# Another order of the operations of the first 48 steps in a chunked-attention and two-layer rational/ReLU² feed-forward kernel

## The chip, the cores and the metric

The kernel runs on one core of one Trainium2 chip. The metric is the device time of one execution in microseconds. TensorE is called PE in the profile, VectorE DVE, ScalarE ACT, GpSimd POOL and SyncE SP. SP does no arithmetic here: it issues loads and stores. ACT issues a few loads too, on a queue of its own.

## The reference

Attention within chunks of 64 rows over 8 batches, 8 heads, 576 positions and 64 dimensions; its output is laid out as 4608 tokens of 512 values. Then two feed-forward layers with 2048 hidden values each.

```python
scores = scale * np.matmul(q_c, k_c.transpose(0, 1, 2, 4, 3))     # chunks of 64 x 64
scores = scores - np.max(scores, axis=-1, keepdims=True)
attn = np.exp(scores)
attn = attn / (np.sum(attn, axis=-1, keepdims=True) + 1e-09)
out = np.matmul(attn, v_c)
x = out.transpose(0, 2, 1, 3).reshape(B * S, H * D)               # 4608 x 512
h = x @ w_in                                                      # first layer
P = a[0] + a[1] * h + a[2] * h2 + a[3] * h3
Q = 1.0 + np.abs(b[0]) * np.abs(h) + np.abs(b[1]) * h2
x = (P / (Q + 1e-6)) @ w_out
r = np.maximum(x @ w_in2, 0.0)                                    # second layer
result = (s * (r * r) + b2) @ w_out2
```

The feed-forward weights arrive as 64-bit floating-point numbers and are turned into 32-bit ones on the chip.

## The kernel before

Every product of two float32 matrices is made from a high and a low half of each factor, in three terms. The tokens are cut into nine tiles of 512 (x tiles). Attention is worked in tiles of 128 tokens, four to an x tile. A step of the first layer takes one x tile and 128 of the hidden values: 12 matmuls of 128x512 into one PSUM bank (`mm1`, lines 530 to 532, token M), the rational function on that bank (ACT, DVE, POOL), and 12 matmuls into the x tile's four accumulators (`mm2`, line 548, token R). Steps 0 to 7 belong to x tile 0, steps 8 to 15 to x tile 1, then 16 steps of tile 2, 8 more of tile 1 and 8 more of tile 0. Step i uses bank i mod 3 (`h_bank`), so M of a step needs the last read of the step three before it, which is its operation Nc. Some of attention's transposes and products take those same banks, or the accumulators' banks, which the first R (R0) needs empty.

The order in which instructions are issued is a list of tokens written out by hand in the program (`START`, lines 33 to 82), played by `play`: each token calls one function and each engine carries out its own tokens in the order of the list. `START` covers the first 48 steps with everything that must come ahead of them; `LOOP` and `TURN` and a planner follow and aren't touched. The tokens, with the number of the tile, weight or step:

- loads: P (q and k of an attention tile, 2 DMAs), L and o (v, 4 DMAs), Q (q and k in another layout, 16 DMAs), w (the next weight block, 512 KB), x (parameters). On SP, or on ACT's queue where the token ends in A.
- attention tile: T transposes of q and k on PE, then q and k (ACT copies them out); or X, a turn on DVE. S scores (PE); sa to sd maxima and subtractions (DVE); e exponential (ACT); ma, mb, mc sum and reciprocal (DVE); n norm (POOL, or DVE with D); A transposes (PE), a copy (ACT); V product with v (PE); v high half of x (ACT), u low half (DVE). The small letter behind T, S, A, V chooses the banks.
- weight block n: f starts the conversion (ACT: absolute value `w_abs`, line 445, and low word `w_low`, line 449); gPa to gPd on DVE for two blocks together (lines 456, 460, 463); c sum (POOL, line 466); d high half (ACT, line 473); D or G low half (DVE or POOL, line 477). A weight's staging buffer is one of four in turn, so load n+4 waits for c of block n.
- step: M; t, B, p (ACT), r (POOL or DVE), ba, bb (DVE), l and E (ACT: logarithm and exponential), Na, Nb, Nc (DVE), H high half (ACT), y low half (POOL, or DVE with D), R.

Of the kernel before, what the change touches and what calls it, by code (L numbers as in the profile page):

```python
# [139 lines left out]
def tile_chunk_attention__then__rational_ffn__then__relu2_ffn(  # L140
# [1227 lines left out]
    with tc.manual_schedule():  # L1368
# [24 lines left out]
        words, pairs = {}, {}  # L1393
# [219 lines left out]
```

## Time and profile before

| what | us |
|---|---|
| median of 3 runs | 1640.9 (1638.43 to 1640.9) |
| profiled execution, time | 1639.77 |
| profiled execution, span from first to last instruction | 1638.0 |
| PE busy | 1586.5 (97%) |
| DVE busy | 1338.1 (82%) |
| ACT busy | 1128.0 (69%) |
| POOL busy | 608.8 (37%) |

The page cuts the span into 40 slices of about 41 us; each digit is the busy share of a slice in tenths. A timeline row gives start, length, engine, line of the program, operation, output and inputs, and in brackets the idle time ahead of it with what ended that. Rows of SPq and ACTq are issues of DMAs: the length is how long the issuing engine was held.

### The profile page before, as it was taken

How to read it: one execution, taken by the hardware profiler on the slowest of the kernel's cores; microseconds unless marked ns; L12 is line 12 of the kernel's file. 1: busy time of each engine (PE TensorE's matmuls, PEld its weight loads, DVE VectorE, ACT ScalarE, POOL GpSimd, SP SyncE). 2: the span in 40 equal slices, each digit the busy share in tenths (PEclk: the TensorE clock that was granted, in tenths of full speed). 3: DMA queues.
4: the chain of work that ended last, by engine and by line, in shares of the span. 5: the costliest groups of instructions: out<-in, count | busy, mean ns of one | idle time of the engine just before them, and what ended most of it. 6: DMA issues, size and time to landing. Idle time of an engine off the chain costs nothing.

```text
span 1638.0 us, 26407 instructions
## 1 busy us (share of the span) xinstructions
PE 1586.5 (97%) x9068; PEld 1293.9 (79%) x9068; DVE 1338.1 (82%) x2165; ACT 1128.0 (69%) x1909; POOL 608.8 (37%) x513
## 2 busy tenths in 40 slices
PE   4699999999999999999999999999999999999998
PEld 3577887777878888888888788888888888888886
DVE  6899988899888988888779987668867886788676
ACT  5788766667677686867678776657665756676554
POOL 3677565347577676757557510000000000000000
PEclk9799999999999999999999999999999999999999
DMA  9655302344263553625034587865589649666853
GB/s 232 158 158 147 93 1 65 84 113 134 66 167 87 154 141 83 196 65 133 3 123 135 206 272 238 324 231 174 164 208 303 233 130 297 213 220 161 279 169 86
DMA packets 365526, 263.93 MB, mean 161 GB/s; under 512 B 276816, under 2 KB 315728, under 8 KB 364880
## 3 DMA queue, kind: packets, MB, share of 16 engines
q1 hardware_dynamic: 352720, 255.55, 53.0%
q10 hardware_dynamic: 12672, 6.69, 1.5%
q8 instruction: 72, 1.18, 0.3%
q14 instruction: 62, 0.51, 0.1%
HBM read 201.33 MB, written 60.82 MB: 160 GB/s over the span
## 4 chain that ended last, share of the span: by engine, by line
PE 79%; DVE 6%; DMA 4%; ACT 4%; issue 3%; POOL 2%; SPq 2%; ACTq 0%; DVEq 0%; POOLq 0%
PE acc L548 20%; PE ae L1107 16%; PE hA L1046 11%; PE h L530 7%; PE h L532 6%; PE h L531 6%; PE hE L1046 5%; PE hc L1046 3%; PE hc L1107 3%; DMA wst<-in_moe_w_in_dram 1%; SPq L269 1%; DMA vs<-in_v_dram 1%; PE pat L383 1%; DVE ah L679 1%; PE pat L408 1%
## 5 line engine op out<-in xcount | busy, mean ns | idle before, releaser
L1107 PE MATMUL ae<-gs,wo 128*128 128x512 f32 x1152 | 294.0, 391 | 1.7 <-DVE acc L1126 0.7
L548 PE MATMUL acc<-gh,w 128*128 128x512 f32 x1152 | 288.0, 392 | 0.0
L530 PE MATMUL h<-xh,w 128*128 128x512 f32 x640 | 256.1, 400 | 8.9 <-DVE t L683 8.0
L1107 PEld LDWEIGHTS ae<-gs,wo 128*128 128x128 f32 x1152 | 215.8, 188 | 49.5 <-DVE acc L1126 1.1
L531 PE MATMUL h<-xl,w 128*128 128x512 f32 x640 | 251.0, 392 | 0.0
L532 PE MATMUL h<-xh,w 128*128 128x512 f32 x640 | 251.0, 392 | 0.0
L548 PEld LDWEIGHTS acc<-gh,w 128*128 128x128 f32 x1152 | 214.1, 188 | 44.4 <-ACT gh L691 0.2
L637 POOL TENSOR_TENSOR r<-r,ah 128x512 f32<-128x512 f32 x130 | 174.3, 1341 | 77.6 <-ACT r L632 65.0
L1046 PE MATMUL hA<-xs,wi 128*128 128x512 f32 x768 | 195.6, 390 | 0.7 <-ACT g L1057 0.7
L697 POOL TENSOR_TENSOR gl<-t,gh 128x512 fp32r<-128x512 f32 x111 | 147.7, 1333 | 100.0 <-ACT gh L691 58.4
L1046 PEld LDWEIGHTS hA<-xs,wi 128*128 128x128 f32 x768 | 144.1, 188 | 31.8 <-ACT g L1057 1.1
L1085 DVE TENSOR_TENSOR gs<-g,gs 128x512 fp32r<-128x512 f32 x224 | 146.4, 684 | 15.1 <-ACT gs L1081 14.5
L548 PE MATMUL acc<-gl,w 128*128 128x512 f32 x576 | 154.8, 390 | 2.0 <-POOL gl L697 1.9
L1081 ACT ACTIVATE gs<-g 128x512 fp32r<-128x512 f32 x224 | 132.7, 624 | 28.2 <-DVE g L1077 27.8
L530 PEld LDWEIGHTS h<-xh,w 128*128 128x128 f32 x640 | 121.2, 189 | 39.1 <-DVE t L683 12.4
L532 PEld LDWEIGHTS h<-xh,w 128*128 128x128 f32 x640 | 121.0, 189 | 26.0
L531 PEld LDWEIGHTS h<-xl,w 128*128 128x128 f32 x640 | 121.2, 189 | 24.2 <-DVE xl L424 0.3
L623 ACT ACTIVATE t<-h,a_sb 128x512 f32<-128x512 f32 x144 | 111.1, 773 | 38.1 <-PE h L532 18.1
L548 PEld LDWEIGHTS acc<-gl,w 128*128 128x128 f32 x576 | 107.6, 188 | 26.5 <-POOL gl L697 4.2
L679 DVE SCALAR_TENSOR_TENSOR ah<-r,h 128x512 f32<-128x512 f32 x144 | 98.1, 681 | 37.1 <-ACT h L668 35.7
L1128 DVE TENSOR_TENSOR acc<-ae,acc 128x512 f32<-128x512 f32 x112 | 77.0, 689 | 61.3 <-PE ae L1107 60.3
L663 ACT ACTIVATE ah<-r,lnb 128x512 f32<-128x512 f32 x144 | 103.6, 719 | 32.8 <-POOL r L637 26.5
(143 smaller groups left out, 2964.9 us busy)
## 6 DMA issues: line engine op xcount, KB each, us to landing
wi<-wq SPq DMA_DIRECT2D x112, 512.0 KB, 4.3
wo<-wq SPq DMA_DIRECT2D x112, 512.0 KB, 4.8
wst<-in_moe_w_in_dram SPq DMA_DIRECT2D x28, 512.0 KB, 5.3
wst<-in_moe_w_out_dram SPq DMA_DIRECT2D x27, 512.0 KB, 4.7
wi<-wp SPq DMA_DIRECT2D x16, 512.0 KB, 4.0
wq<-wc SPq DMA_DIRECT2D x32, 256.0 KB, 2.8
w<-wi SPq DMA_DIRECT2D x16, 512.0 KB, 6.6
raw<-x2d SPq DMA_DIRECT2D x16, 512.0 KB, 7.4
```

The source lines that it names most:

```text
L530: T.matmul(h, wh, xh[:, kk], start=kk == 0, stop=False)
L531: T.matmul(h, wh, xl[:, kk], start=False, stop=False)
L532: T.matmul(h, wl, xh[:, kk], start=False, stop=kk == KD - 1)
L548: T.matmul(o, l, r, start=first and n == 0, stop=last and n == 2)
L623: A.activation(t1, h_t[i], AF.Identity, scale=a_sb[:, 3:4], bias=a_sb[:, 2:3])
L637: eng.tensor_tensor(out=r, in0=r, in1=ah, op=ALU.mult)
L679: V.scalar_tensor_tensor(out=t, in0=r, scalar=ONE, in1=y, op0=ALU.add, op1=ALU.mult)
L697: (eng or (G if i < N1 else V)).tensor_tensor(out=gl, in0=tmp.pop(i)["g"], in1=f(g_t[i][0]), op=ALU.subtract)
L1046: T.matmul(ps[b], w[:, l, z * P:(z + 1) * P], x[:, z], start=n == 0 and p in (1, 2, 5), stop=n == 5, skip_group_check=True)
L1081: A.activation(gx[t, s, k][0][:, 0], gt[t, s, c], AF.Copy)
L1085: V.tensor_tensor(out=g[:, 1], in0=gt[t, s, c], in1=f(g[:, 0]), op=ALU.subtract)
L1107: T.matmul(o, w[:, e, l, dp * P:(dp + 1) * P], gx[t, 2 * u + e, k][0][:, g], start=n == 0 and p in (1, 2, 5), stop=n == 5, skip_group_chec ...
```

## The change

The list `START` is replaced by another. Both name the same operations on the same data. The new one begins with attention tiles 2, 3, 4, 0, 1 where the old one begins with 4, 1, 3, 2, 5, 0. It puts other loads on ACT's queue (w0, w9, w10, L2, L4, L0, P3, P6, P7 where the old one has w1, w6, w27 to w30, L1, L3, L2 and P7), and chooses anew which steps' and tiles' n, r, y, D and G run on which engine, and which banks attention's products use. A new token, h with a letter b, does the low word `w_low` of a weight block by itself; f then does the absolute value alone. For the second layer's weights f does both, as before. The heads of both lists, up to some tokens behind R3:

```diff
-    "w0 w1A f0 P4 w2 f1 P1 g1Pa g1Pb g1Pc c0 d0 T4a L1A T1x q1 k1 g1Pd D0 f2 S1y s1b c1 d1 w3 q4 s1d s1a k4 w4 w5 "
-    "f3 P3 S4b s1c e1 s4b g3Pa g3Pb s4d T3d G1 g3Pc g3Pd m1a c2 m1b m1c P2 f4 c3 n1D f5 w6A d2 g5Pa P5 q3 s4a g5Pb "
-    "P0 d3 s4c w7 g5Pc x0 e4 m4a g5Pd A1a k3 T2b c4 c5 a1 V1a S3x q2 s3b k2 d5 s3a d4 G3 s3c S2b s3d e3 w8 v1 D4 "
-    "s2b L4 u1 T5d s2a G2 k5 G5 q5 L3A T0x q0 w9 s2c k0 S5a m4b S0x m4c s2d s5a n4 s5b f6 m3a P6 m3b A4d a4 s5c w10 "
-    "s0a m3c s0b s5d f7 V4d s0d L0 g7Pa n3 f8 g7Pb g7Pd s0c e2 e5 A3b m5a P7A e0 f9 a3 g7Pc v4 T6b m0a q6 m5b g9Pa "
-    "m5c V3c k6 c6 g9Pb n5D m2a w11 g9Pc m0b u4 m0c w12 n0D w13 Q8 c8 A5b S6a s6b L5 L2A c7 L6 T7b w14 d6 a5 w15 "
-    "m2b d7 v3 m2c k7 q7 g9Pd s6a c9 s6d s6c e6 D7 m6a A0d u3 a0 d8 w16 Q9 d9 n2 S7b m6b G6 A2a a2 V2a s7a m6c f10 "
-    "v2 u2 V0c v0 L7 G8 f11 u0 M0 w17 f12 g11Pa o8 M1 o9 g11Pb w18 f13 g11Pc G9 g11Pd t0 n6 c11 w19 g13Pa B0 c10 p0 "
-    "r0h Q10 A6c d11 M2 s7b w20 b0a g13Pb t1 B1 p1 W0 b0b X8 b1a l0 V5a r1h E0 g13Pc s7c c12 s7d b1b e7 t2 S8b M3 "
-    "N0a d10 l1 d12 s8a G11 a6 G12 m7a v5 B2 N0b f14 m7b E1 D10 N0c m7c b2a u5 n7 A7x b2b g13Pd r2 H0 s8b V6a M4 "
-    "N1a s8d y0 f15 N1b v6 s8c l2 N1c t3 u6 H1 c13 g15Pa E2 b3a Q11 R0 B3 d13 N2a e8 a7 y1 g15Pb N2b D13 M5 N2c r3 "
-    "B4 X9 p4 r4h t4 b3b R1 l3 M6 g15Pc g15Pd c14 H2 l4 y2 E3 f16 b4a N3a f17 b4b E4 N3b V7y c15 B5 p5 r5h m8a d14 "
-    "G14 N3c g17Pa H3 t5 d15 B6 l5 y3 v7 R2 N4a N4b m8b t6 N4c g17Pb o10 b5a m8c b5b E5 n8 u7 g17Pd A8c c17 p6 r6h "
-    "N5a a8 H4 N5b w21A M7 f18 l6 Q12 B7 f19 d17 S9y o11 D15 N5c g17Pc y4D c16 H5 s9a b6a s9c g19Pa b6b G17 s9b E6 "
-    "R3 d16 p7 r7h g19Pb t7 y5D M8 g19Pc R4 t8 N6a b7a N6b s9d B8 X10 G16 l7 b8a N6c f20 f21 r8 o12 R5 g19Pd M9 c19 "
...
+    "w0A P2 w1 L2A T2d P3A k2 q2 w2 S2b w3 f0 f1 T3b s2a s2c h1b s2b s2d e2 g1Pa h0b P4 g1Pb m2a k3 f2 q3 g1Pc f3 "
+    "m2b m2c S3a h2b c0 n2D A2c a2 V2x g3Pa d0 s3a h3b g1Pd v2 T4b g3Pb P0 u2 c1 T0d g3Pd d1 s3b s3c s3d G0 w4 D1 "
+    "q4 k4 S4y w5 c3 k0 e3 q0 f4 f5 h5b P6A g3Pc s4b g5Pa s4d d3 g5Pb s4a P1 P5 s4c T1c e4 g5Pd D3 m3a x0 w6 S0b "
+    "T5d s0b s0a s0c s0d k1 q1 h4b m4a c2 d2 k5 T6a P7A q5 c5 S1x w7 m4b d5 k6 G2 m3b g5Pc w8 f6 m4c q6 n4D s1a s1b "
+    "s1c c4 S5x s1d d4 w9A G5 L3 f7 m3c g7Pa s5a g7Pb e1 n3D h6b L4A G4 g7Pc A4d e0 f8 h7b h8b Q8 a4 g7Pd m0a s5b "
+    "c6 c7 m0b m1a s5c f9 s5d A3y V4y m0c m1b w10A e5 g9Pa d7 a3 L0A V3a g9Pb m1c g9Pd n0D w11 g9Pc c8 n1D L1 h9b "
+    "v3 m5a A0b d6 a0 d8 w12 c9 G7 G6 d9 m5b w13 v4 V0a L5 Q9 A1b u3 w14 w15 v0 L6 X8 u4 T7x D8 w16 w17 a1 m5c f10 "
+    "n5 f11 w18 q7 V1b o8 v1 A5x k7 u0 h11b a5 f12 g11Pa S6a G9 h10b u1 g11Pb f13 g11Pd g11Pc c11 c10 w19 h12b s6b "
+    "M0 s6a s6d M1 t0 g13Pa s6c b0a B0 V5y e6 g13Pb S7a S8b p0 r0h o9 m6a L7 w20 B1 p1 b0b m6b g13Pc t1 v5 l0 E0 "
+    "m6c h13b d10 r1h c12 b1a d11 Q10 u5 b1b g13Pd l1 s8a M2 E1 t2 B2 N0a n6 s7b N0b N0c c13 N1a G10 H0 s7d d13 G11 "
+    "A6c f14 f15 h15b b2a N1b W0 s7a G13 N1c s7c H1 p2 r2h g15Pa e7 y0D g15Pb b2b X9 M3 m7a t3 M4 B3 y1 l2 p3 r3h "
+    "a6 Q11 E2 d12 V6a g15Pc v6 b3a f16 o10 l3 b3b m7b B4 N2a Q12 m7c s8b N2b N2c f17 E3 g15Pd G12 u6 s8d t4 n7 "
+    "h16b h14b N3a r4 A7x s8c N3b g17Pa c14 b4a c15 N3c M5 h17b l4 e8 R0 H2 b4b m8a y2D B5 R1 E4 p5 r5h t5 g17Pb H3 "
+    "N4a b5a m8b g17Pd g17Pc N4b l5 d14 a7 y3D c17 b5b d15 N4c M6 c16 m8c B6 t6 p6 r6h E5 b6a H4 n8 R2 y4 d16 G16 "
+    "d17 b6b D14 M7 l6 R3 w21A f18 f19 E6 t7 B7 N5a D15 N5b N5c V7c f20 N6a D17 R4 N6b v7 A8y f21 h20b N6c u7 H5 M8 "
...
```

```diff
-    def w_ends(st, w):
-        w_abs(st, w)
-        w_low(st)
...
-            w_ends(st, w)
+            w_abs(st, w)
+            if phase:
+                w_low(st)
...
-        do["h"] = lambda n, _: w_get(n)
+        do["h"] = lambda n, x: w_low(words[n][3]) if x else w_get(n)
```

## Rows read from the trace of the kernel before

**Rows 1.** The page: busy time of each engine, and PE in tenths of 40 slices
```profile
PE 1586.5 (97%) x9068; PEld 1293.9 (79%) x9068; DVE 1338.1 (82%) x2165; ACT 1128.0 (69%) x1909; POOL 608.8 (37%) x513
...
PE   4699999999999999999999999999999999999998
```

**Rows 2.** Busy time by stretch: stretch, length, each engine, clock, DMA share, GB/s
```profile
0.00:20.00 20.00, 6.62 (x80) 4.76 (x80) 5.83 (x13) 9.53 (x17) 4.82 (x9) 1.00 1.02 245
20.00:60.84 40.84, 24.85 (x425) 19.40 (x425) 36.58 (x76) 28.28 (x58) 22.93 (x18) 0.80 0.80 202
60.84:96.79 35.95, 29.53 (x201) 23.17 (x201) 32.72 (x58) 30.12 (x54) 25.67 (x20) 0.85 0.55 129
96.79:205.00 108.21, 106.60 (x706) 86.66 (x707) 102.09 (x170) 88.92 (x153) 76.56 (x62) 1.00 0.47 134
205.00:600.00 395.00, 389.75 (x2569) 316.11 (x2568) 340.93 (x566) 277.64 (x463) 251.73 (x217) 1.00 0.40 103
```

**Rows 3.** Timeline of PE, 0 to 100 us: start, length, line, output<-input, count [wait <-releaser]
```profile
7.90 2.13 PE L316 MATMUL pat<-ident,qk 128*128 128x128 f32 x8 [7.90 <-DMA qk<-in_q_dram]
...
18.45 1.14 PE L339 MATMUL pat<-qk,vq 64*64 64x64 f32 x32 [1.48 <-ACT qk L320]
...
53.25 1.09 PE L316 MATMUL pat<-ident,qk 128*128 128x128 f32 x8 [1.57 <-ACT eT L393]
...
60.84 0.79 PE L530 MATMUL h<-xh,w 128*128 128x512 f32 x1 [0.80 <-ACT xh L416]
...
65.63 0.39 PE L530 MATMUL h<-xh,w 128*128 128x512 f32 x1
...
77.43 0.79 PE L530 MATMUL h<-xh,w 128*128 128x512 f32 x1 [3.41 <-DVE t L683]
...
85.12 0.50 PE L530 MATMUL h<-xh,w 128*128 128x512 f32 x1 [1.53 <-DVE t L683]
...
87.98 1.98 PE L548 MATMUL acc<-gh,w 128*128 128x512 f32 x8
...
90.70 0.39 PE L530 MATMUL h<-xh,w 128*128 128x512 f32 x1
...
96.79 0.50 PE L530 MATMUL h<-xh,w 128*128 128x512 f32 x1 [0.49 <-DVE t L683]
```

**Rows 4.** Timeline of the issues on SP, 0 to 100 us
```profile
1.77 0.57 SPq L253 DMA_DIRECT2D qk<-in_k_dram  x1
2.39 3.96 SPq L436 DMA_DIRECT2D wst<-in_moe_w_in_dram  x1
...
79.16 3.90 SPq L269 DMA_DIRECT2D qk<-in_k_dram  x8
```

**Rows 5.** Timeline of ACT and of the issues on its queue, 0 to 100 us
```profile
0.76 0.49 ACTq L436 DMA_DIRECT2D wst<-in_moe_w_in_dram  x1
...
11.69 2.97 ACTq L282 DMA_DIRECT2D vq<-in_v_dram  x4
...
40.96 0.37 ACTq L253 DMA_DIRECT2D qk<-in_q_dram  x1
41.37 0.87 ACTq L253 DMA_DIRECT2D qk<-in_k_dram  x1
```

**Rows 6.** Timeline of DVE, 0 to 100 us
```profile
17.07 0.42 DVE L349 TENSOR_REDUCE mx<-pat 128x4 f32<-128x256 f32 x1 [3.62 <-PE pat L339]
```

**Rows 7.** Groups of DVE by line, 17 to 165 us: count, busy us, mean ns, idle before
```profile
L463 DVE SCALAR_TENSOR_TENSOR w<-wst,w 128x512 int32<-128x512 int32 x22 | 18.2, 841 | 0.1
...
L683 DVE SCALAR_TENSOR_TENSOR t<-t,a_sb,h 128x512 f32<-128x512 f32 x15 | 11.1, 741 | 0.2
...
L477 DVE TENSOR_TENSOR w<-w,w 128x512 fp32r<-128x512 f32 x7 | 7.6, 1091 | 0.2 <-ACT w L473 0.2
...
L349 DVE TENSOR_REDUCE mx<-pat 128x4 f32<-128x256 f32 x20 | 8.0, 414 | 5.7 <-PE pat L339 4.7 <-PE h L339 1.0
```

67 rows, old and new, of the table START are left out of this document.

## The prediction

> **What bounds the kernel now.** I read the page first [rows 1]: TensorE (PE) is busy 97% of the span, and only the first two of its 40 slices are far from full. So a new order of the first 48 steps can win only what PE loses near the start. Then the stretches [rows 2]: up to 60.84 us PE is busy 6.62 + 24.85 us, up to 96.79 us 29.53 more, so 35.8 us of the first 96.79 are idle, and the granted clock there is 0.80 and 0.85 of full. From 96.79 to 205 us PE idles 1.6 us and from 205 to 600 us 5.25 us. Everything that can be won lies ahead of 97 us, and at most 7 us behind it.
>
> The timeline of PE tells what ends the idle time [rows 3]. Step 0's first product (M0) starts at 60.84, when the fourth of x tile 0's four attention tiles has left ScalarE (ACT) and VectorE (DVE). After that PE waits for DVE three times: M3 3.41 us (77.43), M4 1.53 us, M6 0.49 us (96.79), each time for the last DVE operation (token N..c) of the step three back, because a step's product needs one of three PSUM banks. DVE is busy 36.58 of 40.84 us and 32.72 of 35.95 us [rows 2], so from 20 us on DVE is the bound, and what it misses it misses ahead of 20 us (5.83 of 20 us busy); its attention work starts at 17.07 [rows 6].
>
> **Yardstick.** Behind M6 PE is full in both lists, so the end moves by what PE has lost when that state is reached: clock time less the PE work done, at full clock. Full-clock prices: an M or R is 2.73 us (R0 runs from 87.98 to 90.70 [rows 3]), a T 1.1 (53.25), S, A and V 0.65, 0.45 and 0.6. Ahead of M6 the old list has 6 M, 2 R, 8 T, 9 S, 8 A, 7 V = 44.2 us, so it has lost 96.79 - 44.2 = 52.6 us.
>
> **DVE's share of the lists.** DVE's prices, start to start (row mean less about 0.07 of overlap with the next [rows 7]): a maximum or subtraction of S 0.345, a step operation 0.62 to 0.67, a weight's top half 0.78, a low half 1.03, other weight operations 0.61 and 0.64; attention's sums 1.1 in three parts, norms 0.9, the low half of x 0.67, a turn of q and k 1.21. Up to N3c, which frees M6's bank, the old list has 132 tokens = 73.1 us, where rows 2 measure 5.83 + 36.58 + 32.72 = 75.1; the idle rest of 96.79 is 21.7. In the new list the tight place is N2c, which frees M5's bank: 123 tokens = 67.6 us, with 36.1 us of PE work ahead of M5 (the old list puts R0 and R1 ahead of M6, the new one puts M5 ahead of R0). DVE work less PE work is 31.5 in the new list against 28.9 in the old: the new list leans on DVE 2.6 us more there, and wins only if DVE idles less than 21.7 - 2.6 = 19.1 us on the way.
>
> **DVE's idle time in the new list, token by token.** I go along the new list with these prices, every engine in its order.
> - Start. The first loads are P2 (q and k of tile 2) on SP at 0.74 and 1.2, with w0 and L2 on ACT's queue. The old P4 lands for 7.90 behind one weight on its own queue and beside one on the other [rows 3]; P2 has none ahead on its own. I take q at 5.2 and T2 done at 8.5 (half-clock T: 2.13 us, S 1.14 [rows 3]). ACT issues w0A, L2A, P3A first: 0.49 + 2.97 + 1.24 (0.37 and 0.87) [rows 5], free near 6.4; until 8.5 it has nothing to do, so these issues cost nothing. The second half of P3A could be held by a full queue like SP's fourth issue, 3.96 us, or go like the one before it, 0.57 [rows 4]; I take 1.6 between these ends, nearer the lower, since one weight's and one v load's bytes are ahead where SP had a weight's and a q's and k's. Then k2, q2, S2: DVE starts at 10.65, not 17.07.
> - Tile 2: maxima to 12.1, e2, norm to 15.9, A2 and V2 at half clock, v2 at 19.3: DVE waits 1.25 us for it. T4 and T0 at half clock end at 22.9, q0 leaves at 24.5, and S4 needs q0's bank: wait 2.0. Tile 0's maxima end at 32.2. P6A is issued at 26 to 28, lands near 32, T6 and S1 end at 35.5: wait 0.3.
> - ACT then sets the pace: P7A and w9A put f7 at 38.3 (wait 1.25), L4A puts e0 at 42.8 (wait 0.4), L0A puts v3 at 51.5 and v4 at 54.15 (wait 0.7). ACT's list up to v1 is 68 activations of 0.50 (37.8 us for 75 in rows 2) = 34 us and 9 issues = 14.1 us, 48 in all; the old one to its last v is 71 and 11.1, 46.7.
> - Q8's 16 issues (3.90 us for 8 [rows 4]) move on SP ahead of w11, L1, w12 and w13 and end near 47; w11 is wanted at 55.8 and V1 at 55, so 5 us of cover hides them. Without the cover M0 moves one for one.
> - u1 ends at 58.1, M0 starts at 58.5 (2.3 us earlier). At half clock it takes about 4.8 us, as the old M0 did (60.84 to M1's start at 65.63 [rows 3]), so t0 is late and DVE waits 1.9. N0c comes at 73.3 (in time for M3 at 73.4, old 77.43), N1c at 76.5, N2c at 86.0.
>
> Idle: 10.65 + 1.25 + 2.0 + 0.3 + 1.25 + 0.4 + 0.7 + 1.9 = 18.4, and 67.6 + 18.4 = 86.0. Between N1c and N2c lie 9.4 us of DVE work; PE has M4, V6 and A7 there, idles some 5 us in two parts, and M5 comes at low clock as M3 did (4.8 us) or not (2.73). R0 also needs s8c, 2.8 us behind N2c. So R0 starts at 88.8 to 90.8, with 38.8 us of PE work done: lost 50.0 to 52.0, against 52.6. Gain 0.6 to 2.6; less the 2.0 us by which the old list's means fell short of its measured busy time, if that recurs, it is -1.4 to 2.6. Splitting the weights' low word from the absolute value (h tokens) adds no instruction and only lets it stand later. Which steps' norms and low halves run on GpSimd and which on DVE is in the 67.6. The waits behind 97 us (6.9 us) I leave as they are: their places differ, nothing in the trace says they fall or grow.
>
> I take a gain of 1.3: against the profiled execution (1639.77 us, of which 1638.0 are span) that is 1638.5; the median of the runs shown lies 1.1 higher.
>
> **A rule that speaks against part of it.** The DMA engines are full in the first 20 us: share 1.02, 245 GB/s [rows 2]. The Trainium skill, "DMA: Bandwidth & Descriptors", section "Issuing engines are not separate DMA queues", says that loads issued from several engines run on the same 16 engines, and that a second issuer only saves the issue time. The trace agrees as far as that share goes; by the rule, P3, P6, L4 and L0 on ACT bring nothing sooner in total and leave only their cost on ACT, which is the second rival.
>
> **Rivals.**
> 1. More gain. The waits of 2.0, 1.25 and 1.9 rest on half-clock prices. If PE keeps full clock from 20 us on (T 1.1, S 0.65, M0 2.73), some 4 of those 5 us go, M5 is not slowed, and the lost time is about 46 to 48: gain 4 to 8, 1632 to 1636. For it: both clocks occur in rows 3; with all 6.9 us of later waits gone too it would be 1630 at best. Against: the stretch from 20 to 60.84 has clock 0.80.
> 2. ACT becomes the bound: slower. Three v loads and three q/k loads stand on ACT, and its list to v1 is 48 us against 46.7. If P3A holds ACT as long as SP was held (3.96 us [rows 4]), k2 slips from 8.5 to about 10 and the low cover on ACT passes every later microsecond of L4A and L0A to v3, u1 and M0. From 2 us of such delay on the gain is gone; at 4 to 7 us the time is 1642 to 1645.
> 3. It washes out: M0 comes earlier, and the DVE-heavy piece ahead of N2c, or a wait for a GpSimd norm, gives it back: 1639 to 1641. This is also where the case lies that waits of issues were off the path from the start.
>
> **How the numbers follow.** Forecast 0.42 (1636.5 to 1641.5, nearly all within 0.2%), rival 1 0.31, rival 2 0.17, rival 3 0.10. 0.2% is 3.3 us, about what a measurement of this kernel can tell from no change. Faster by more: rival 1 and a little of the forecast, 0.37. Slower by more: rival 2 with the tail of rival 3, 0.18. The same: 0.45. The range goes from rival 1's best, 1630, to rival 2's 1645, which leaves out about 0.15.
>
> **What would show it.** DVE's first maximum near 10.7 us, M0 near 58.5, a wait of M5 for DVE of 3 to 5 us, R0 near 89 to 91. ACT held more than 3 us at its second P3 issue, or M0 behind 61, would show rival 2; R0 ahead of 87 with clock 1.0 from 60 us on would show rival 1. The working is wrong if PE still waits for anything but DVE between M2 and R1, or if the later waits change by more than 3 us.

## The result, and the profile after

The changed kernel takes 1649.28 us (median of 6 runs, 1646.7 to 1651.16) where the kernel before takes 1640.47 beside it (6 runs, 1638.43 to 1641.69): a ratio of 1.0057 [1.0047, 1.0067], some 9 us slower. Forecast were 1638.5 us and a range that ended at 1645. The profiled execution of the changed kernel took 1648.24 us, 1646.4 of them span, against 1639.77 and 1638.0.

Busy time by stretch, with the columns of [rows 2] and the same stretches:

```profile
0.00:20.00 20.00, 6.51 (x80) 4.74 (x80) 6.53 (x14) 7.90 (x13) 1.99 (x7) 1.00 1.04 230
20.00:60.84 40.84, 20.11 (x322) 16.66 (x315) 30.65 (x64) 24.82 (x50) 19.93 (x15) 0.71 0.82 195
60.84:96.79 35.95, 27.60 (x289) 21.51 (x288) 34.66 (x67) 32.80 (x62) 26.13 (x21) 0.86 0.42 113
96.79:205.00 108.21, 104.55 (x690) 85.13 (x689) 95.43 (x160) 85.68 (x148) 81.81 (x68) 0.98 0.50 135
205.00:600.00 395.00, 388.44 (x2565) 316.02 (x2564) 332.51 (x551) 275.37 (x460) 252.65 (x217) 1.00 0.39 101
```

Against [rows 2], the loss lies between 20 and 60.84 us: PE has done 20.11 us instead of 24.85 there, DVE 30.65 instead of 36.58, ACT 24.82 instead of 28.28. All three engines did less at once, so they waited for something outside them. Behind 96.79 us PE idles 3.66 + 6.56 us where it idled 1.61 + 5.25: 3.4 us more.

The timeline of PE (start, length, line, output and input, wait and releaser), to be laid beside [rows 3]:

```profile
51.08 1.09 PE L384 MATMUL pat<-ident,e 128*128 128x128 f32 x4 [8.91 <-DVE sm L372]
...
65.65 0.50 PE L527 MATMUL h<-xh,w 128*128 128x512 f32 x1
...
68.71 0.39 PE L527 MATMUL h<-xh,w 128*128 128x512 f32 x1
...
80.11 0.50 PE L527 MATMUL h<-xh,w 128*128 128x512 f32 x1 [1.08 <-DVE t L680]
...
88.64 1.13 PE L409 MATMUL pat<-eT,vq 64*64 64x64 f32 x32 [2.39 <-ACT eT L394]
92.13 1.11 PE L384 MATMUL pat<-ident,e 128*128 128x128 f32 x4 [2.36 <-POOL e L378]
...
96.76 1.98 PE L545 MATMUL acc<-gh,w 128*128 128x512 f32 x8
```

M0 starts at 65.65 (forecast 58.5, before 60.84 [rows 3]), M1 at 68.71, R0 at 96.76 (forecast 88.8 to 90.8). From M0 to R0 it is 31.1 us, as forecast (30.3 to 32.3). So what R0 lacks was lost ahead of M0.

What held M0 is on ACT. Its timeline with the issues on its own queue (ACTq; the length is how long ACT was held):

```profile
1.29 5.61 ACTq L283 DMA_DIRECT2D vq<-in_v_dram  x4
6.94 0.62 ACTq L254 DMA_DIRECT2D qk<-in_q_dram  x1
8.36 0.38 ACTq L254 DMA_DIRECT2D qk<-in_k_dram  x1
...
40.62 0.66 ACT L450 ACTIVATE wst<-wst 128x512 int32<-128x512 uint32 x1
45.23 2.66 ACTq L283 DMA_DIRECT2D vq<-in_v_dram  x4
47.93 0.63 ACT L363 ACTIVATE e<-e 128x512 f32<-128x512 f32 x1 [6.65 <-DMA vq<-in_v_dram]
...
52.21 4.87 ACTq L283 DMA_DIRECT2D vq<-in_v_dram  x4
57.12 0.65 ACT L450 ACTIVATE wst<-wst 128x512 int32<-128x512 uint32 x1 [4.32 <-DMA vq<-in_v_dram]
```

At 45.23 stands L4A, at 52.21 L0A. ACT has nothing running from 41.28 to 47.93: it stands in front of L4A's first issue for 4 us and then issues for 2.66. The chain of work that ended last (start, length, what) shows whom it stood for:

```profile
36.89 1.29 POOL w L463
38.18 0.02 issue
38.20 0.38 SPq L437
38.58 0.05 issue
38.63 0.72 SPq L283
39.35 0.05 issue
39.41 5.80 DMA vq<-in_v_dram
45.20 0.02 issue
45.23 0.65 ACTq L283
```

GpSimd's c4 frees a staging buffer, SP issues w8 into it, then L3, which stood behind w8; one of L3's DMAs lands at 45.20, and only then does ACT's issue of L4A go, 0.03 us later. ACT's queue waited for a load of SP's queue. The same chain shows it at the start: P3A's second issue on ACT goes at 8.36, when the first load of L2A has landed.

```profile
1.29 7.05 DMA vq<-in_v_dram
8.34 0.02 issue
8.36 7.78 DMA qk<-in_k_dram
```

It is the program that makes its loads wait, and the trace shows how. Each load tells of its landing on one of eight marks (semaphores) that both queues share, and none of the changed kernel's 74 loads issued in the first 62 us goes before the load that last used its mark has landed. 17 of them go within 0.1 us behind that landing, 6 of these among the 21 on ACT's queue; in the kernel before it is 12 of 64, and 1 of 16 on ACT's (one mark's landings can't be read there). So at most eight loads are under way at a time, whatever their size (512 KB for a weight block, 32 KB for one of Q8's), and an engine whose next instruction is a load stands until its mark is free.

Behind ACT stood e0, behind e0 DVE's sums of tile 0, behind these A0 on PE. DVE's largest wait between its start and N2c, and its busy time up to there (in the last row, behind PE's and PEld's):

```profile
48.59 0.69 DVE L369 TENSOR_REDUCE sm<-e 128x8 f32<-128x512 f32 x1 [4.22 <-ACT e L363]
...
0.00:92.22 92.22, 49.65 (x665) 39.10 (x666) 67.47 (x134) 60.95 (x114) 45.10 (x39) 0.83 0.75 180
```

N2c ends at 92.22. DVE has worked 67.47 us by then, forecast were 67.6; it has idled 24.75, forecast were 18.4, and 19.1 was the most with which the new list would still win.

### The profile page after: what moved, and what is told of

The parts are those of the page before. It is cut to its first block, busy times and chain, and to the rows that moved or that the text cites. A ratio compares the mean times of both kernels' runs of the same rounds, so it can differ in the third digit from the quotient of the medians.

```text
span 1646.4 us, 26424 instructions
## 1 busy us (share of the span) xinstructions
PE 1584.8 (96%) x9068; PEld 1296.0 (79%) x9068; DVE 1330.3 (81%) x2155; ACT 1128.7 (69%) x1909; POOL 619.5 (38%) x523
## 4 chain that ended last, share of the span: by engine, by line
PE 81%; DMA 4%; DVE 4%; POOL 3%; ACT 3%; issue 2%; SPq 2%; ACTq 0%; DVEq 0%; POOLq 0%
PE acc L545 21%; PE ae L1104 16%; PE hA L1043 11%; PE h L527 7%; PE h L528 7%; PE h L529 7%; PE hE L1043 5%; PE hc L1043 3%; PE hc L1104 2%; DMA vq<-in_v_dram 1%; PE pat L409 1%; PE pat L384 1%; POOL r L634 1%; SPq L270 1%; POOL r L631 1%
## 5 line engine op out<-in xcount | busy, mean ns | idle before, releaser
L694 POOL TENSOR_TENSOR gl<-t,gh 128x512 fp32r<-128x512 f32 x117 | 155.3, 1329 | 91.4 <-ACT gh L688 55.2
L620 ACT ACTIVATE t<-h,a_sb 128x512 f32<-128x512 f32 x144 | 111.2, 773 | 27.7 <-POOL gl L694 13.1
L545 PEld LDWEIGHTS acc<-gl,w 128*128 128x128 f32 x576 | 107.6, 188 | 27.0 <-POOL gl L694 4.7
L660 ACT ACTIVATE ah<-r,lnb 128x512 f32<-128x512 f32 x144 | 103.7, 720 | 31.1 <-POOL r L634 27.4
```

Source lines behind the costliest of these rows:

```text
L545: T.matmul(o, l, r, start=first and n == 0, stop=last and n == 2)
L620: A.activation(t1, h_t[i], AF.Identity, scale=a_sb[:, 3:4], bias=a_sb[:, 2:3])
L660: A.activation(tmp[i]["ah"], tmp[i]["r"], AF.Ln, scale=RS, bias=lnb)
L694: (eng or (G if i < N1 else V)).tensor_tensor(out=gl, in0=tmp.pop(i)["g"], in1=f(g_t[i][0]), op=ALU.subtract)
```

## The experiments

Theory A: what is lost is lost ahead of M0, where ACT, and through it DVE and PE, waits for loads to land. Theory B, B2: the order of work between N1c and R0 sets R0, whatever M0 does. Others came up on the way: the waits behind R2 (e7, e8), the split of the low word (e11), the weights' late start (theory D, e17). Each kernel was timed four to six times beside the kernel before. In the table, M0, N2c's end and R0 are from the one profiled execution, "rest" is that execution's own time less its M0, and DVE's idle time up to N2c stands where the operations up to there are the changed kernel's.

| kernel | ratio to before | M0 | N2c | DVE idle | R0 | rest |
|---|---|---|---|---|---|---|
| before | 1 | 60.84 | | | 87.98 | 1578.9 |
| e16: before, L4 on ACT | 1.0036 [1.0024, 1.0049] | 66.83 | | | 92.25 | 1577.8 |
| changed | 1.0057 [1.0047, 1.0067] | 65.65 | 92.22 | 24.8 | 96.76 | 1582.6 |
| e1: L4 on SP | 1.0045 [1.0031, 1.0060] | 62.99 | 92.51 | 25.1 | 97.06 | 1583.8 |
| e2: L4, L0 on SP | 1.0053 [1.0039, 1.0066] | 68.10 | 94.85 | 29.2 | 100.71 | 1582.4 |
| e3: P3A first | 1.0058 [1.0045, 1.0071] | 68.83 | 95.29 | 29.1 | 101.16 | 1582.7 |
| e4: L3 ahead of w8 | 1.0057 [1.0044, 1.0069] | 67.80 | 94.34 | 28.5 | 98.92 | 1582.7 |
| e9: Q8 late | 1.0070 [1.0058, 1.0083] | 66.40 | 96.30 | 30.8 | 101.27 | 1585.8 |
| e11: no split | 1.0063 [1.0050, 1.0076] | 66.67 | 93.73 | 27.7 | 98.35 | 1583.5 |
| e13: v loads early | 1.0056 [1.0043, 1.0070] | 64.28 | 90.80 | 24.5 | 95.44 | 1581.9 |
| e17: weights first | 1.0063 [1.0051, 1.0075] | 67.64 | 94.20 | 26.9 | 98.70 | 1582.5 |
| e7: new, old behind R2 | 1.0057 [1.0043, 1.0071] | 65.81 | 92.65 | 25.6 | 98.42 | 1580.9 |
| e8: old, new behind R2 | 1.0112 [1.0099, 1.0126] | 60.59 | | | 86.67 | 1595.4 |
| e5: N2, M5 early | 1.0096 [1.0082, 1.0110] | 64.95 | 89.03 | | 96.90 | 1587.8 |
| e6: e5, L4 on SP | 1.0088 [1.0074, 1.0102] | 64.77 | 90.7 | | 98.85 | 1588.1 |
| e10: tile 7 early | 1.0070 [1.0057, 1.0084] | 68.69 | 96.0 | | 99.27 | 1587.0 |
| e12: e10, L4 on SP, Q8 late | 1.0063 [1.0050, 1.0076] | 63.65 | 90.3 | | 93.61 | 1586.9 |
| e14: e10, step 3 in its order | 1.0106 [1.0090, 1.0123] | 66.76 | 94.0 | | 97.32 | 1590.6 |
| e15: e14 with e13's loads | 1.0109 [1.0095, 1.0123] | 63.93 | 91.3 | | 96.16 | 1593.5 |
| e18: e1, weights behind R0 | 1.0087 [1.0073, 1.0101] | 66.28 | 89.5 | | 92.39 | 1586.3 |

Two things stand in the last column. As long as the order behind M0 is the new list's (changed, e1 to e4, e11, e13, e17), the rest is 1581.9 to 1583.8, though M0 moves by 6 us: the end follows M0 one for one. And the kernels whose lists are the same up to M0 (changed, e5, e7, e10, e14) start it at 64.95 to 68.69, so one profile tells M0 only to some 4 us. Taken together, that list starts M0 at 66.4 on average, the one with L4 on SP (e1, e6, e18) at 64.7, the one with three v loads early (e13, e15) at 64.1. So ACT's v loads may be worth some 2 us of the 7 that M0 is late; with so few profiles and this spread it isn't shown.

**e16: one v load of the kernel before on ACT.**

```diff
-    "s2b L4 u1
+    "s2b L4A u1
```

> The kernel before with one load moved: tile 4's v load (L4) from SP to ACT's queue at its place in the list. Theory A (a v load on ACT at this place holds ACT until earlier loads of SP have landed, and ACT's work for attention stands behind it): ACT held 3 to 6 us more near 47 us, M0 2 to 4 us later than 60.84, time 1642 to 1645. If a v load on ACT costs only its own issue time: M0 within 1 us, 1640 to 1641.5.

1646.07 us against 1639.35: 5.9 us by the ratio, more than expected, and M0 6.0 us later (e8, whose head is the old one with the low words split off, has M0 at 60.59, as the kernel before). The hold came at 37 to 41 us, not near 47. Its rows on ACT, DVE and PE, and the chain at the hold:

```profile
37.66 3.80 ACTq L281 DMA_DIRECT2D vq<-in_v_dram  x3
41.51 0.60 ACT L319 ACTIVATE vq<-pat 128x512 f32<-128x512 f32 x1 [4.38 <-DMA vq<-in_v_dram]
...
44.93 0.42 DVE L355 TENSOR_TENSOR e<-pat,mx 128x256 f32<-128x256 f32 x1 [5.33 <-PE h L382]
...
66.83 0.51 PE L529 MATMUL h<-xh,w 128*128 128x512 f32 x1 [1.08 <-ACT xh L415]
```

```profile
33.32 4.32 DMA vq<-in_v_dram
37.64 0.02 issue
37.66 3.84 DMA vq<-in_v_dram
```

L4A stands ahead of L3A on ACT's queue here. L3A's second issue goes at 37.66, when L4A's first load, issued at 33.32, has landed, and L3A's last three issues take 3.80 us where one alone took 0.60. ACT idles 4.38 us ahead of the copy behind them, DVE waits 5.33. A load that a compute engine issues is paid by everything that stands behind it on that engine: theory A's mechanism, in a list where nothing else was changed.

**e1, e2, e4, e9: ACT's loads given to SP, or SP's loads ahead of them moved.**

```diff
e1
-    "... e1 n3D h6b L4A G4 ..."
+    "... e1 n3D h6b L4 G4 ..."
e2: e1 and
-    "... d7 a3 L0A V3a ..."
+    "... d7 a3 L0 V3a ..."
e4
-    "... g5Pc w8 f6 ... w9A G5 L3 f7 ..."
+    "... g5Pc L3 w8 f6 ... w9A G5 f7 ..."
e9
-    "... h8b Q8 a4 ... w13 v4 V0a L5 Q9 A1b u3 w14 w15 v0 L6 X8 u4 ... B0 V5y ..."
+    "... h8b a4 ... w13 v4 V0a Q8 L5 Q9 A1b u3 w14 w15 v0 L6 u4 ... B0 X8 V5y ..."
```

> The new list with one token changed: the four loads of tile 4's v (L4) are issued by SP instead of ACT, at the same place of the list. Theory A (ACT is held by its own issues): in the new list ACT stood idle from 41.3 to 45.2 us ahead of these four issues and was held 2.7 us by them, DVE waited 4.2 us for the exponential behind them. Without them DVE's wait at 48.6 shrinks by some 4 us, M0 (65.65) starts 3 to 4 us earlier, and the time falls by 3 to 4 us, to about 1645. Theory B (the DVE-heavy piece between N1c and N2c is the bound): M0 earlier, but M5 and the time within 1 us of the new list's 1649.

> The new list with two tokens changed: the v loads of tiles 4 and 0 (L4, L0) on SP instead of ACT. ACT was held 4.9 us by L0 (52.2 to 57.1) and DVE waited 1.9 us behind it. Theory A: M0 5 to 6 us earlier than 65.65, time 1643 to 1645, that is 2 us more gain than with L4 alone. Theory B: no more than 1 us of gain. A third possibility: v of tile 0 then stands behind 16 issues of Q8 on SP, lands too late for its product, and M0 is no earlier than with L4 alone.

> The new list with the four loads of tile 3's v (L3) moved ahead of weight load w8 on SP; L4 stays on ACT. In the new list ACT's first L4 issue began at 45.23, when L3's first load landed. If the wait was for L3's data or its place behind w8, it goes: L4 is issued from 41.3, the time falls 3 to 4 us. If it comes from landing marks that the loads of both queues share in turn (the program has ACT's four issues wait for loads issued on SP: here w8 and three of Q8's), ACT is held until these have landed, about 43 to 47 us, and the time changes by less than 1.5 us.

> Only Q8 (16 loads) and the turn X8 that reads it are moved: Q8 on SP from behind L3 to behind w13, X8 to ahead of V5. Theory A (loads in flight hold ACT: its issues of L0A wait for landings of earlier loads of SP): L0A is no longer held near 52 us, ACT's 4.3 us wait there falls below 2, M0 starts 1 to 3 us earlier than 65.7. Theory B2 (what sets R0 is the meeting of N2c, tile 6's and tile 7's chains near 92 us, which hangs on DVE's, ACT's and GpSimd's order): R0 stays within 1 us of 96.8 and the time within 2 us of the changed kernel's, 1646 to 1650. Theory A alone: R0 near 94 to 95 and 1645 to 1647.

In e1 ACT no longer stands for L4A, and M0 came 2.66 us earlier, which is within the spread named above; but ACT waits 2.01 us for a weight at 43.99 and 5.13 us for L0A at 54.32, and R0 comes no earlier. In e2 L0 stands on SP behind Q8 (issued at 57.04), and ACT waits 7.05 us in front of 63.52. In e4 L3 is issued from 33.69 on, and still L4A's first issue goes only at 46.04 and ACT idles 6.76 us up to 50.13. So of the two causes named beforehand it is the shared marks, not L3's data or its place behind w8. In e9 L0A is held 5.62 us without Q8 in front of it. None of them has less DVE idle time up to N2c than the changed kernel (25.1 to 30.8 against 24.8), and the intervals of all four ratios overlap its interval. Where a wait was taken away, one for another load came in its place.

**e13: three v loads early.**

```diff
-    "... S4y w5 c3 ... L3 f7 ... L4A G4 ... a3 L0A V3a ..."
+    "... S4y L3 L4 L0 w5 c3 ... f7 ... G4 ... a3 V3a ..."
```

> The three v loads L3, L4 and L0 are issued on SP ahead of w5, in the stretch of 17 to 23 us in which SP waits for a staging buffer and the DMA share is 0.7 to 0.8; none of them is on ACT any more, and none on SP behind w8 or Q8. Nothing else is moved. Theory A (the landings that ACT's issues wait for are the loss ahead of M0): the idle times of ACT near 48 and 57 us are gone, M0 at 59 to 61 instead of 65.7. If that is also what sets R0: R0 at 91 to 92.5, time 1643 to 1645. Theory B2 (the meeting of N2c with the chains of tiles 6 and 7 takes the gain back, as it did when L4 alone was moved): R0 no earlier than 94, 1646 to 1649.

ACT's idle times at 48 and 57 us are gone as expected, and M0 is at 64.28, not at 59 to 61. The rows show the exchange, SP's issues first, then DVE (here L445 and L452 are the lines of `w_abs` and of a weight's first operation on DVE):

```profile
18.42 8.33 SPq L282 DMA_DIRECT2D vq<-in_v_dram  x12
...
32.26 0.70 DVE L452 TENSOR_SCALAR w<-w 128x1024 f32<-128x1024 f32 x1 [3.06 <-ACT w L445]
...
46.02 0.69 DVE L452 TENSOR_SCALAR w<-w 128x1024 f32<-128x1024 f32 x1 [3.09 <-ACT w L445]
```

The twelve v issues take SP until 26.85, 0.69 us each, w5 goes then instead of at 23.03, and DVE waits 3.06 and 3.09 us for weights instead of 4.22 for e0. DVE's idle time is 24.5, the changed kernel's is 24.8. So no one of these loads is what is late; the delay passed to others.

**e3 and e17: the first 20 us.** e3 issues P3A ahead of L2A; e17 converts the first two weights ahead of tile 2, as the kernel before does with tile 4.

```diff
e3
-    "w0A P2 w1 L2A T2d P3A k2 q2 ..."
+    "w0A P2 w1 P3A L2A T2d k2 q2 ..."
e17
-    "w0A P2 w1 L2A T2d P3A k2 q2 w2 S2b w3 f0 f1 T3b s2a s2c h1b s2b s2d e2 g1Pa h0b P4 g1Pb ... c0 ... g1Pd ... c1 ..."
+    "w0A P2 w1 P3A f0 T2d f1 k2 q2 L2A h0b w2 S2b w3 T3b g1Pa g1Pb g1Pc s2a s2c h1b s2b s2d e2 c0 g1Pd P4 c1 ..."
```

> The new list with ACT's first two loads exchanged: q and k of tile 3 (P3) ahead of v of tile 2 (L2). In the new list ACT was held 5.6 us by L2's four issues, P3 was issued at 6.9 and 8.4 and landed at 13.9 and 16.2, and the conversion of weights 2 and 3 stood behind it (DVE waited 1.8 us at 19.6). If the late P3 costs what the working missed there, T3 comes 3 to 5 us earlier, DVE idles 1.5 to 3 us less by 20 us, and the time falls by 1.5 to 3 us, to 1646 to 1648. If the later waits behind ACT's issues swallow it, the time stays at 1649 within 1 us.

> Theory D: the loads behind 17 us run late because SP stands at w5 until 23 us for a staging buffer, and that is free only when GpSimd's c1 is done (21.3 to 23.0; c0 at 15.9 to 17.2), since the new list starts DVE on attention and does the first two weights' g1 behind it. Here the first two weights are converted ahead of tile 2's maxima, as the kernel before does (f0, f1 ahead of k2 and behind q2, g1 ahead of s2, c0 and c1 right behind; L2A is issued behind q2); the rest of the list is the new one. Theory D expects c1 done by 18, w5 issued by 18 to 19, DVE's first work at 8 to 9 us and its idle time up to N2c 3 to 6 us below the changed kernel's 25, M0 at 60 to 63, R0 at 91 to 94, 1643 to 1646. If the wait moves again to another load, as in e1, e9 and e13: M0 at 63 to 66, R0 at 96 to 98, 1646 to 1650. If L2A's later issue holds ACT in tile 2's chain: 1649 to 1652.

Both missed. In e3 it is L2A that is held, longer than before:

```profile
2.66 9.89 ACTq L283 DMA_DIRECT2D vq<-in_v_dram  x4
12.66 0.60 ACT L321 ACTIVATE qk<-h 128x512 f32<-128x512 f32 x1 [10.64 <-DMA wst<-in_moe_w_in_dram]
```

ACT comes to its first copy at 12.66 instead of 9.24. In e17 c1 is done at 19.1 and w5 issued at 19.10 (23.03 in the changed kernel), but f1 has to wait for w1 until 11.54, DVE starts at 12.22, and c4 and so w8 come no earlier (39.39; 38.20). So the staging buffer that SP waits for at 23 us isn't what makes the rest late.

**e7 and e8: the lists cut at R2 and crossed, with the low words split off throughout.**

```diff
e7
-    "<new list to R2> <rest in the new order>"
+    "<new list to R2> <rest in the old order>"
e8
-    "<old list to R2> <rest in the old order>"
+    "<old list to R2> <rest in the new order>"
```

> The new list up to R2 (about 108 us), then what is left in the order of the old list. It prices the head alone. By the two traces the head has lost 5.4 us more than the old one by the first R (R0 at 96.8 with 38.8 us of PE work done, where the old one reached M6 at 96.8 with 44.2 done), and the waits behind 100 us cost 3.4 more. So if the two pieces are independent: 1645 to 1647, and no wait of PE at 142 us. If the waits behind 100 us are caused by the state in which the head leaves the loads, 1648 to 1650.

> The old list up to R2, then what is left in the order of the new list. If the new order behind R2 is itself worse (its o8 and Q10 stand on SP behind the weights 16 to 18, which wait for staging buffers), the time is 2 to 4 us above the kernel before, 1642 to 1645, with PE waiting near 135 to 145 us. If the new tail is as good as the old one: 1640 to 1641.5.

e7 has the whole loss: 1.0057, the changed kernel's ratio. PE idles less behind 96.79 us, 2.98 + 4.25 us against 3.66 + 6.56, but R0 is 1.7 us later though the lists agree up to there. By the last column the tail adds 1.7 us by itself (1582.6 against 1580.9); a difference of that size can't be told by these intervals. e8 says nothing on the tail: at the seam a product of attention waits 4.65 us for a step's bank, and a step's M 6.20 us for that product's low half.

```profile
103.41 0.37 PE L408 MATMUL h<-eT,vq 64*64 64x64 f32 x2 [4.65 <-DVE t L679]
...
115.41 0.79 PE L526 MATMUL h<-xh,w 128*128 128x512 f32 x1 [6.20 <-DVE xl L424]
```

**e11: the split undone.**

```diff
-            if phase:
-                w_low(st)
+            w_low(st)
...
-    "... T3b s2a s2c h1b s2b s2d e2 g1Pa h0b P4 ..."
+    "... T3b s2a s2c s2b s2d e2 g1Pa P4 ..."
```

> One part of the change undone: f does the absolute value and the low word together again, the h tokens are gone; everything else is the new list. The prediction took the split at nothing. If so, 1647 to 1650. If the search leaned on it (low words stand up to some 10 tokens later), ACT has 0.6 us more ahead of several of attention's copies: 1650 to 1654. If the split costs, 1644 to 1647.

1650.84 us, a ratio of 1.0063 against 1.0057: no cost of the split shows, and no gain.

**e5, e6, e10, e12, e14, e15, e18: another order between N1c and R0.** The segment of the new list, and three of its orders (e6 is e5 with L4 on SP; e12 is e10 with L4 on SP and Q8 late; e15 is e14 with e13's loads; e10 is e14 but for b3a, b3b and N3, which stand behind E3 and behind the weight work, so that in e10 and e12 the polynomial of step 3 is made from the exponential's values, which the reference doesn't do; they stand here for the order's time alone):

```diff
-    "A6c f14 f15 h15b b2a N1b W0 s7a G13 N1c s7c H1 p2 r2h g15Pa e7 y0D g15Pb b2b X9 M3 m7a t3 M4 B3 y1 l2 p3 r3h a6 Q11 E2 d12 V6a g15Pc v6 b3a f16 o10 l3 b3b m7b B4 N2a Q12 m7c s8b N2b N2c f17 E3 ... A7x s8c ... N3c M5 h17b l4 e8 R0"
e5
+    "... N1c s7c p2 r2h b2b l2 E2 H1 g15Pa g15Pb N2a N2b N2c e7 y0D X9 M3 m7a t3 M4 ... s8b M5 f17 E3 ... A7x ... R0"
e14
+    "A6c b2a p2 r2h N1b W0 s7a G13 N1c s7c b2b e7 l2 y0D a6 E2 H1 M3 V6a M4 t3 f14 f15 h15b g15Pa m7a m7b m7c n7 g15Pb N2a N2b N2c M5 B3 p3 r3h v6 b3a A7x u6 s8b s8d s8c b3b l3 E3 R0 ..."
e18 (on e1)
+    "A6c b2a p2 r2h N1b W0 s7a G13 N1c s7c e7 l2 y0D b2b M3 E2 a6 M4 H1 t3 B3 m7a m7b m7c n7 y1 V6a A7x N2a N2b N2c M5 p3 r3h v6 u6 s8b s8d s8c b3a l3 b3b E3 B4 R0 f14 f15 h15b ..."
```

> Theory B says that what sets the first R in the new list is the stretch between N1c and M5: l2, E2 and N2a to N2c stand behind a transposition on DVE, a norm's sums, and other steps' operations, and M5 stands behind N3c and behind A7, which waits for a norm on GpSimd. Here l2, E2 and N2a to N2c come right after N1c, and M5 right after tile 7's scores instead; L4A stays on ACT. Theory B expects M5 near 88 us instead of 92.9, R0 near 91 to 93 instead of 96.8, and a time 3 to 5 us below the changed kernel, 1644 to 1646. Theory A (ACT held on its loads is the whole loss, and passes to everything behind it) expects M0 at 65.7, R0 within 1 us of 96.8 and 1648 to 1650.

> The same move of N2 and M5 with tile 4's v load on SP. Alone that load's move brought M0 forward by 2.65 us and R0 by nothing. Theory B expects that now M0's gain is kept: M0 near 63, R0 near 88 to 91, 1641 to 1643. If a third limit binds (loads that come late on SP for the weights, between 60 and 75 us) R0 stays near the one of the run without L4's move, and the time is 1644 to 1646. Theory A expects what the load's move alone gave, 1647 to 1648.

> In the changed kernel three chains end together just ahead of R0: N2c at 92.2, tile 7's norm on GpSimd at 92.1 (A7 waits for it, and tile 8's subtractions behind A7, and R0 behind those), and V6 at 88.6, which waits for a6 on ACT. Moving N2 alone left R0 at 96.9, because V6 and A7 came later. Here all three come earlier: e7, l2, a6, E2 right behind N1c on ACT, m7 and n7 right behind, then N2, M5, and tile 8's subtractions and R0 ahead of the work for steps 3 and 4. Theory B2 expects M5 at 86 to 89, R0 at 90 to 93 and a time 3 to 6 us below the changed kernel's, 1642 to 1646, unless steps 3 to 5, whose operations now stand behind, give it back. Theory A: R0 within 1 us of 96.8.

> The reordering of e10 with tile 4's v load on SP and Q8 late as well: both causes at once. If the head loses by both, M0 near 61 to 63, M5 near 84 to 87, R0 at 88 to 90 and 1638 to 1643, near the kernel before. If the loads that now come late on SP, or steps 3 to 6 behind R0, take the gain: 1645 to 1650.

> The reordering of e10 between N1c and R0 again, now with step 3's b3a and b3b ahead of E3 and its N3 ahead of weight and turning work (in e10 and e12 the polynomial of step 3 read its bank after the exponential had overwritten it, and N3c came late: M6 waited 2.5 us for it). Loads as in the changed kernel. Theory B2: R0 near 92 to 94 and M6 within 6 us of R0, time 1643 to 1646. Theory A: R0 within 1 us of 96.8, 1648 to 1650.

> e13 and e14 together. If the loss ahead of R0 is made of these two limits, each of which holds R0 when the other is lifted, the whole of it comes back only here: M0 at 59 to 61, R0 at 86 to 89, time 1637 to 1642. If a third limit stands behind them, R0 stays above 91 and the time above 1644.

> Both limits again, on the list with tile 4's v load on SP (e1), and this time without f14, f15, h15b, g15, X9, f16 and d12 ahead of the chains (in e10, e14 and e15 DVE stood 2.6 us at g15Pa for f15's result): p2 ahead of N1b, then e7, l2, E2, a6 on ACT, m7, n7 and N2 right behind on DVE and GpSimd, V6, A7, M5 and tile 8's subtractions behind them, and the weight work behind R0. Compared with e1 only this order differs. If the order between N1c and R0 is what took L4's gain back: N2c near 88 to 90 instead of 92.5, R0 at 91 to 93 instead of 97.06; the time 3 to 6 us below e1's, 1642 to 1645, provided that the weight work put behind R0 doesn't hold M7. If it does, R0 is earlier, but M7 stays near 108 and the time within 2 us of e1's. If R0 doesn't move although these chains come first, it is DVE's total of work and idle time up to there that sets it.

All are slower than the changed kernel or not told from it. In e5 N2c is 3.2 us earlier and V6 then waits 5.75 us for ACT's a6; in e10, e14 and e15 DVE waits 2.6 us at g15Pa for f15. e18 does most plainly what was meant: R0 at 92.39, 4.4 us earlier than in the changed kernel although M0 is no earlier. It still takes 1653.64 us, and PE's rows behind R0 show where that went:

```profile
92.39 2.06 PE L545 MATMUL acc<-gh,w 128*128 128x512 f32 x8
...
104.75 3.78 PE L545 MATMUL acc<-gh,w 128*128 128x512 f32 x8 [3.93 <-ACT gh L688]
...
112.24 0.50 PE L527 MATMUL h<-xh,w 128*128 128x512 f32 x1 [2.01 <-DVE t L680]
```

R2 waits 3.93 us, M7 starts at 112.24 (107.6 in the changed kernel): the weight work put behind R0 now stands ahead of them. Theory B2 falls: the order between N1c and R0 does set R0, but it isn't where the time is lost. None of these orders is better there than the new list's, and how early R0 comes tells nothing of the end if the work that it passed is still owed.

## Why the prediction was wrong

Take its time as M0 plus the rest: 58.5 + 1580.0 forecast, 65.65 + 1582.6 in the profiled execution. The miss of 9.7 us is 7.15 at M0 and 2.6 behind it.

- **What bounds the kernel, and DVE's share: right.** The gain had to come ahead of 97 us, and the loss came there. DVE's work up to N2c was 67.47 us against 67.6, and the condition (DVE idle below 19.1) tells the sign correctly with the idle time of 24.75: 5.65 us too much.
- **Idle time ahead of L4A: right as a sum.** 15.8 us measured (10.68 + 1.81 + 1.65 + 1.63) against 15.45. The start was 0.9 us late (11.58 against 10.65), and not for P3A, which was in doubt in the text, but for P2: its k let the second half of T2 start only at 8.09, and T2 ended at 9.2 instead of 8.5. ACT's issues didn't matter there. L2A held ACT 5.61 us instead of 2.97, and P3A took from 6.94 to 8.74, 1.8 us for the 1.6 taken, but the first copy, at 9.24, waited for T2.

```profile
8.09 1.11 PE L317 MATMUL h<-ident,qk 128*128 128x128 f32 x4 [0.59 <-DMA qk<-in_k_dram]
...
9.24 0.60 ACT L321 ACTIVATE qk<-h 128x512 f32<-128x512 f32 x1 [7.23 <-PE h L317]
```

- **The step that failed: "L4A puts e0 at 42.8 (wait 0.4), L0A puts v3 at 51.5".** Both loads were priced at 2.97 us, the length of the row at 11.69 [rows 5] (the "9 issues = 14.1 us" hold it three times), and the wait for an earlier load's landing at nothing. The issuing itself was priced right: L4A's four issues took 2.66 us. The wait wasn't. ACT came to L4A at 41.28, 2.1 us later than the 39.2 that 42.8 leaves when that issue and e0 are taken off; it lost 6.65 us there (3.7 over the price) and 4.32 at L0A (1.35 over). That makes the 7.15 by which M0 was late. The exact agreement is luck: e0 ended 5.8 us late (48.56) and v3 6.8 (58.3). The rows had a warning, SP's fourth issue of 3.96 us [rows 4]; the prediction used it as a bound for P3A alone and for no later load. e16 shows the size in the kernel before: 5.9 us for one such load. What isn't shown is that these two terms alone make the loss. e2 and e13 took the two loads off ACT, M0 came at 68.10 and 64.28, and waits for other loads stood in their place. So the wait that the prediction put at nothing is one of the whole stream of loads, not of L4A and L0A only.
- **M0 at half clock: wrong, and it didn't matter.** M0 took 3.1 us at a granted clock of 1.00 (4.8 us at 0.58 before), with PE busy without a pause from 60 us on, and DVE's wait of 1.9 us behind it was below 0.6. "Half-clock" for the first transposes is read off their length alone: the granted clock is 1.00 in the first 20 us [rows 2], though eight of them took 2.13 us there and 1.09 us at 53.25 [rows 3].
- **From M0 to R0: right in sum, in part by luck.** It is 31.1 us, and M3 waits for N0c, but later by M0's delay. M0 took 1.7 us less than taken, and M2 waited 2.42 us for u5, which wasn't in the working. PE's wait ahead of M5 is 4.75 us in two parts, as was said, and in the 3 to 5 that were named, but not for DVE: the parts are for ACT's a6 and for GpSimd's n7. N2c came at the same time as n7 (92.22; A7 starts at 92.13), so R0 lost little by it. The line "wrong if PE still waits for anything but DVE" caught this.
- **"The later waits I leave as they are": wrong by 3.4 us.** PE idles 10.2 us from 96.79 to 600 us, against 6.9. One place is seen. SP stands 20.86 us at weights 16 to 18, and Q10, which stands behind them, is issued from 108.32 on (97.16 before). The turn X10, which reads it, comes at 123.92 (114.75), Q11 goes into the buffer that X10 leaves, at 125.25, and X11 waits 3.16 us for Q11's k (the row names a v load that landed beside it). PE waits 0.84 + 1.88 us around 143 to 146.

```profile
76.96 20.86 SPq L437 DMA_DIRECT2D wst<-in_moe_w_in_dram  x3
...
142.23 0.71 DVE L328 STREAM_TRANSPOSE qkT<-qk 128x512 f32<-128x512 f32 x1 [3.16 <-DMA vs<-in_v_dram]
...
145.66 0.69 PE L409 MATMUL pat<-eT,vs 64*64 64x64 f32 x32 [1.88 <-issue]
```

That this order costs the 2.6 us is argued: e7, with the old order behind R2, idles 3.0 us less behind 96.79, but its ratio is the changed kernel's.

- **The rivals.** Rival 2 had the mechanism (ACT held by its loads, M0 behind 61) and the sign; it had the wrong place, P3A instead of L4A and L0A, and with 1642 to 1645 it stopped at the delay's own price, without the waits behind R0. Rival 1's condition, full clock from 20 us on, didn't come: the granted clock was 0.71 from 20 to 60.84 us, with PE busy 20.11 of 40.84. Rival 3 is out by M0, which came later, not earlier.
- **The rule that spoke against part of it.** The Trainium skill, "DMA: Bandwidth & Descriptors", section "Issuing engines are not separate DMA queues", says that issuing from several engines saves only the time of issuing. e13 agrees: it gave L3 and ACT's L4 and L0 an earlier place on SP, and DVE's idle time stayed at 24.5 us. What the prediction added to it, that the cost stays on ACT, came true at a higher price than its own: e16 paid 5.9 us for one load.

Theory A holds for the place of the loss (M0) and, by e16, for the way in which a load on ACT costs time. That ACT's loads are the loss in the new list isn't shown: taking them off ACT gave back nothing that can be told.

What stays open: why the stream of loads is late in the new list. M0 came no earlier than 62.99 in any of its variants. The one staging buffer of e17 isn't it. Two limits are seen, and no run varied either alone: full DMA engines (their share was 0.94 while ACT stood ahead of L4A's first issue, 41.28 to 45.23, and 0.94 again at L0A, but 0.57 from 44 to 52 us), and the eight marks, of which a load of 32 KB takes one as a load of 512 KB does.

## What to carry to other kernels

Price a load that a compute engine issues by the landing that it may have to stand for (here ACT lost 4.3 to 6.65 us at one of four DMAs), not by the length of a free issue (2.6 to 3.0), and list what is queued behind it on that engine. Count the marks on which a program's loads tell of their landing: they bound the loads under way. Look for the milestone with which the end moves one for one (here M0); a milestone that work was merely moved past, as R0 in e18, says nothing. Before two kernels are compared by it, see how far it moves by itself (here some 4 us). When loads are issued in one full stream, moving one load forward can move another back; count the idle time of the engine that they feed, not the wait that went away.

## What the runs showed that was not expected

An issue on ACT's queue waited for a load of SP's queue: L3's DMA landed at 45.20 and L4A went at 45.23. The four issues of a v load took between 2.58 us (SP, at 97.87) and 9.89 us (ACT in e3), so the length of one row says little.

The issuing alone isn't free either: with no wait to speak of, twelve v loads took SP 8.33 us in e13, 0.69 us each, and what stood behind them, w5, went that much later.
